# Loading v through a cast into SBUF per row tile, and the weights in ten pieces, in a top-k attention and MLP-mixer kernel

## The chip, the cores and the metric

The kernel runs on one core of a Trainium2 chip. The metric is device time in microseconds of one execution: 942.34 us is the median of three runs of the kernel before (939.85, 942.34 and 950.61). Profiles are of one execution each, on that core.

## What is computed

Eight batches of eight heads, 576 rows, 64 columns a head, in float32. Each row of scores keeps its 32 largest entries; the rest are masked out before the softmax. The attention output (576 x 512 per batch) goes through an MLP mixer.

```python
scores = scale * np.matmul(q, k.transpose(0, 1, 3, 2))
kth = np.partition(scores, -top_k, axis=-1)[..., -top_k:-top_k + 1]
scores = np.where(scores >= kth, scores, -1000000000.0)
attn = np.exp(scores - np.max(scores, axis=-1, keepdims=True))
attn = attn / (np.sum(attn, axis=-1, keepdims=True) + 1e-09)
x = np.matmul(attn, v)          # (8, 8, 576, 64), then (8, 576, 512)
h = np.maximum(x.transpose(0, 2, 1) @ w_tok1, 0.0) @ w_tok2
u = x + h.transpose(0, 2, 1)
out = u + np.maximum(u @ w_ch1, 0.0) @ w_ch2
```

## The kernel before

**Units and tiles.** The work is cut into 32 units; a unit is one pair of heads of one batch, four units make a batch. The 576 rows are four full row tiles of 128 and one of 64; with two heads a unit has nine score tiles of 128 x 576 (the two short ones share a tile). They are worked on in two groups, g=0 with four tiles and g=1 with five.

**One unit.** q and k are loaded in float32 on SP's DMA queue (`load_one`, L280; the first unit's k on ScalarE's), transposed on TensorE (`qk_tr`, L308), copied by ScalarE (`qk_ev`). Score products follow (`s1_mm`, `s0_mm` L360 to L372, `st_mm`), ScalarE copies them to SS (L375 and others). VectorE then selects the 32nd largest of each row. It splits the 576 columns into maxima and minima of halves (`upper`, L406, then `split4`, L430 to L440), takes the top eight again and again (`top_round`, MAX8 at L451 and MATCH_REPLACE8 at L456), and ends with `low_round` (L470). Beside it GpSimd rebuilds the smaller half from integer bits in two steps (`both_bits` L413, `lower_bits` L421), which `low_round` needs. GpSimd also does the small `neg_max` (L496), `raise_kth` (L522, tile kbig), `keep_ends` (L478, L479), and `sink` (L536), which masks four of the nine tiles in place.

**From scores to O.** The masked tiles have to be transposed before the product with v. Four of a unit's tiles (0, 1, 4, 5) are "turned": ScalarE makes a steep mask (`steep`, L528), GpSimd subtracts it, ScalarE takes the exponential into a buffer pb (L510), and a DMA transpose on SP's queue turns it (`turn`, L541). The other five are transposed by TensorE products with an identity (L558 and L561) and copied out by ScalarE (L581 to L614). Then `o_mm` (L620 to L632) makes O = P v for each head; v has a column of ones, so O's last column is the softmax denominator. VectorE takes its reciprocal (`o_den`, L638), and ScalarE or VectorE scales O into Xb (L648, L657). O has one bank, so the second head's product waits for the first head's scaling.

**The mixer.** After each unit the token mixing follows for its 128 channels (`h1_mm` L668, `ut_mm` L689). After each batch come the hidden products (`h2_mm` L723, `h2t_mm` L739, against wc1b) and the output products (`out_mm` L764, against wc2b), evacuated by ScalarE (L730, L745, L772) and stored by SP (L778). They are spread among the units of the next batch. The last batch has its own version (L1109 on).

**v and the weights.** For each batch one DMA on GpSimd's queue casts v from DRAM to a bf16 copy v16 in DRAM (`vconv`, L302); for each unit three DMAs on SP bring the pair's part of it into one of three buffers vb. The weights are cast into SBUF by GpSimd DMAs (`plan_weights`, L792): w1 and w2 together, wc1 in two halves of 768 KB, wc2 in two halves of 768 KB, each tied to the end of GpSimd's bit steps of an early half-unit (L911 to L914).

**What sets the order.** Each engine works through its instructions in program order. That order is made when the kernel is built: `Plan` (L36) simulates the engines with a fixed cost for each task (`dur`), waits (`deps`), buffers (`acq`, `rel`) and extra delays (`slack`); of the tasks that are ready on an engine it takes the one with the smallest `prio`, which is the unit's number times 100 plus an entry of `RANK` (L19). Entries ending in `_wait` are delays in tenths of a microsecond. `port` marks tasks that it keeps from running at once on VectorE and GpSimd. Where it finds TensorE idle it adds unread products into a free bank (`spare`, L265, 0.22 us planned for each 512 columns, L106 to L116):

```python
at, r, i = min(idle) if idle else (now, "", 0)
n = int((now - at) * SPARE / SPARE_US)
```

The times of the plan are not measured times; only the order of the instructions goes into the program.

## Time and profile before

| what | value |
| --- | --- |
| median of three runs | 942.34 us (939.85 to 950.61) |
| the profiled execution's own time | 944.13 us |
| its span, first to last instruction | 942.3 us |
| TensorE, VectorE, ScalarE, GpSimd busy | 861.9, 847.6, 846.3, 659.0 us |
| mean granted clock of TensorE | 0.973 |
| DMA queue of SP | 203,920 packets, 53.42 MB, 27.7% of 16 engines' span |
| DMA queue of GpSimd | 3,376 packets, 8.46 MB, 5.6% |

PE is TensorE, PEld its weight loads, DVE VectorE, ACT ScalarE, POOL GpSimd, SP SyncE; a q behind a name is that engine's instruction queue. `out<-in` names tiles written and read. In a timeline a row has the start, the length, the instruction and, in brackets, how long the engine stood idle before it and what ended that. In the chain of waits a row has the start, the share of the path in us, and what it was spent on. In a table by stretches each engine has its busy time and, in parentheses, the instructions that touch the stretch; then come the granted clock, the share of the DMA engines and GB/s. A group's row has count, busy time and mean (or shortest, median and longest) duration in ns.

### The profile page before, as it was taken

The numbers are of one execution on the slowest core, as the hardware profiler recorded it, in microseconds if no ns is written. First come the engines' busy times: TensorE is split into PE (matmuls) and PEld (weight loads), VectorE is DVE, ScalarE is ACT, GpSimd is POOL, SyncE is SP. The second block draws the span as 40 slices with busy tenths as digits, with TensorE's granted clock in tenths as the row PEclk, the third lists the DMA queues.
The fourth block names the chain that finished last, engine by engine and source line by source line (L and its number), as shares of the span: only waits on it lengthen the run. The fifth ranks groups of instructions, "written<-read, shape, count | busy, mean of one in ns | idle before, by whom it ended". The sixth has DMA issues, their size and how long they took to land.

```text
span 942.3 us, 22686 instructions
## 1 busy us (share of the span) xinstructions
PE 861.9 (91%) x7559; PEld 486.3 (52%) x7660; DVE 847.6 (90%) x3767; ACT 846.3 (90%) x1873; POOL 659.0 (70%) x542
## 2 busy tenths in 40 slices
PE   8979999899998999899998999899998999989896
PEld 6657555445553555455554455545554555545452
DVE  3987999899997999979997999979998899999852
ACT  3786899899998999899998999989998999999772
POOL 1984767788686778858677777867678577785800
PEclk9998999999998999899998999989998999999999
DMA  3494823334332232413324233412325232121101
GB/s 76 80 126 96 114 42 80 66 71 95 66 65 42 66 82 64 86 36 79 85 53 73 65 83 78 77 30 65 98 60 75 50 75 63 42 33 43 55 15 54
DMA packets 208621, 63.70 MB, mean 68 GB/s; under 512 B 200752, under 2 KB 203120, under 8 KB 208240
## 3 DMA queue, kind: packets, MB, share of 16 engines
q1 hardware_dynamic: 203920, 53.42, 27.7%
q0 software_dynamic: 3376, 8.46, 5.6%
q8 instruction: 62, 1.02, 0.4%
q14 instruction: 63, 0.52, 0.2%
q10 hardware_dynamic: 1200, 0.30, 0.2%
HBM read 40.50 MB, written 14.16 MB: 58 GB/s over the span
## 4 chain that ended last, share of the span: by engine, by line
ACT 41%; PE 23%; DVE 19%; POOL 11%; issue 3%; DMA 2%; ACTq 0%; DVEq 0%; SPq 0%
ACT U L528 6%; ACT SS L375 5%; ACT E L510 5%; DVE A L451 5%; PE s L365 5%; POOL kbig L522 4%; ACT pb L510 4%; ACT U L552 4%; DVE hx L456 4%; ACT pt L581 3%; ACT H2T L730 3%; ACT xb L648 3%; PE mps L764 3%; PE mps L723 3%; DVE A L470 3%
## 5 line engine op out<-in xcount | busy, mean ns | idle before, releaser
L413 POOL TENSOR_TENSOR lo<-SS 128x1152 int32<-128x1152 int32 x64 | 169.0, 2641 | 150.5 <-DVE A L451 132.2
L451 DVE MAX8 A<-hx 128x8 f32<-128x72 f32 (+2 forms) x1152 | 269.6, 292 | 0.0
L456 DVE MATCH_REPLACE8 hx<-A,hx 128x72 f32<-128x72 f32 (+1 forms) x864 | 199.0, 240 | 0.0
L365 PE MATMUL s<-qkT 64*128 64x512 f32 x512 | 171.0, 668 | 4.0 <-ACT SS L355 2.1
L421 POOL TENSOR_TENSOR lo<-lo,hi 128x1152 int32<-128x1152 int32 x64 | 169.2, 2643 | 0.0
L536 POOL TENSOR_TENSOR SS<-SS,U 128x576 f32<-128x576 f32 x126 | 159.1, 1287 | 0.0
L522 POOL TENSOR_SCALAR kbig<-A 128x4 f32<-128x4 f32 (+1 forms) x63 | 101.8, 1616 | 81.3 <-DVE A L470 68.2
L375 ACT COPY SS<-s 128x512 f32<-128x512 f32 x256 | 144.3, 627 | 15.3 <-PE s L365 15.3
L561 PE MATMUL tp<-identN,U 128*128 128x128 bf16 (+1 forms) x810 | 115.9, 220 | 16.1 <-ACT U L552 14.0
L510 ACT ACTIVATE E<-SS,nmax 128x576 bf16<-128x576 f32 x162 | 127.3, 825 | 0.2 <-POOL nmax L496 0.2
L552 ACT ACTIVATE U<-SS,A 128x576 bf16<-128x576 f32 x157 | 126.3, 838 | 0.0
L558 PE MATMUL tp<-identB,E 128*128 128x128 bf16 (+1 forms) x810 | 121.9, 222 | 4.5 <-ACT pt L585 2.0
L558 PEld LDWEIGHTS <-E 128*128 128x128 bf16 (+1 forms) x810 | 78.3, 100 | 77.3 <-issue 67.9
L470 DVE MAX8 A<-lo 128x8 f32<-128x296 f32 x288 | 116.9, 451 | 0.2
L528 ACT ACTIVATE U<-SS,kbig 128x576 bf16<-128x576 f32 x126 | 93.2, 810 | 23.0 <-POOL kbig L522 23.0
L406 DVE TENSOR_TENSOR hi<-SS 128x1152 f32<-128x1152 f32 x64 | 98.1, 1533 | 16.8 <-ACT SS L375 15.0
L723 PE MATMUL mps<-UT,wc1b 128*128 128x512 bf16 x323 | 90.4, 411 | 19.1 <-ACT H2T L745 15.7
L764 PE MATMUL mps<-wc2b,H2T 128*128 128x512 bf16 (+1 forms) x406 | 102.7, 380 | 4.1 <-issue 4.0
L510 ACT ACTIVATE pb<-SS,nmax 128x576 bf16<-128x576 f32 x126 | 102.9, 828 | 0.0
L561 PEld LDWEIGHTS <-U 128*128 128x128 bf16 (+1 forms) x810 | 80.0, 100 | 35.4 <-ACT U L552 26.4
L365 PEld LDWEIGHTS s<-qkT 64*128 64x128 f32 x512 | 54.2, 192 | 53.4 <-issue 31.7
L269 PEld LDWEIGHTS <-identB 128*128 128x128 bf16 x862 | 60.7, 102 | 38.2 <-issue 12.7
(121 smaller groups left out, 1577.5 us busy)
## 6 DMA issues: line engine op xcount, KB each, us to landing
qL<-in_q_dram SPq DMA_DIRECT2D x64, 128.0 KB, 2.6
kL<-in_k_dram SPq DMA_DIRECT2D x62, 128.0 KB, 2.7
out_dram<-ob SPq DMA_DIRECT2D x28, 256.0 KB, 2.3
v<-in_v_dram POOLq DMA_DIRECT2D x8, 576.0 KB, 7.5
vb<-v SPq DMA_DIRECT2D x64, 64.0 KB, 2.3
pt<-pb SPq DMA_TRANSPOSE x126, 2.4
wc1b<-in_moe_w_ch_dram POOLq DMA_DIRECT2D x2, 768.0 KB, 10.6
wc2b<-in_moe_w_ch_dram POOLq DMA_DIRECT2D x2, 768.0 KB, 8.5
```

The costliest lines, as they stand in the source:

```text
L365: nc.tensor.matmul(out=x[:, :], lhsT=T[rows[hh], 0, t * P : (t + 1) * P], rhs=T[rows[hh], 1, 0:W], start=True, stop=True,)
L375: nc.scalar.copy(out=st["SS", t // 2][:, 2 * (t % 2) + hh, 0:W], in_=st["s0", t][hh][:, :])
L413: nc.gpsimd.tensor_tensor(out=x[:, 0:4, 0:HALF].bitcast(i32), in0=SS[:, 0:4, 0:HALF].bitcast(i32), in1=SS[:, 0:4, HALF:S].bitcast(i32), op ...
L421: nc.gpsimd.tensor_tensor(out=x, in0=x, in1=st["hi"][:, 0:4, :].bitcast(i32), op=ALU.subtract)
L451: nc.vector.max(A[:, i, at], hx[:, i, 0:w])
L456: nc.vector.match_replace(hx[:, i, 0:w], A[:, i, TOP[r] : TOP[r] + 8], hx[:, i, 0:w], NEG)
L510: nc.scalar.activation(out=x, in_=srow(st, i), func=AF.Exp, bias=st["nmax", g][:, a : a + 1], scale=scale,)
L528: nc.scalar.activation(out=U[:, :], in_=srow(st, i), func=AF.Relu, bias=st["kbig", g][:, a : a + 1], scale=-STEEP,)
L536: nc.gpsimd.tensor_tensor(out=x, in0=x, in1=st["U", i][:, :], op=ALU.subtract)
L552: nc.scalar.activation(out=U[:, :], in_=srow(st, i), func=AF.Relu, bias=kcol(st, i), scale=-1.0)
L558: nc.tensor.matmul(out=out, lhsT=st["E", i][:, cols], rhs=identB[:, :], start=True, stop=False)
L561: nc.tensor.matmul(out=out, lhsT=st["U", i][:, cols], rhs=identN[:, :], start=False, stop=True)
```

## The change

- v is cast on its way from DRAM straight into SBUF, a row tile for all eight heads at a time (`v_piece`), by five DMAs per batch on GpSimd's queue. The copy in DRAM and the loads on SP go. There are two buffers vb, each for a batch.
- The weights come in ten pieces instead of five: w1 (two DMAs), w2, wc1 in four quarters, wc2 in four quarters, 384 KB each.
- All these DMAs are tied to the end of `upper`, the first step of a half-unit's selection: up to three v pieces of batch 0 and w1 in unit 0, one weight piece per half from unit 1 to unit 5's first half, and one v piece per half in the two units ahead of a batch and its first half.
- They have `port=False`, so the plan lets them run beside VectorE.
- The hidden products wait for wc1's pieces alone, the output products for wc2's.
- `LEAD` (4.6) replaces 0 as the time from which a bank counts as free at the start of the plan.
- Four buffers pb instead of five, one output buffer ob instead of two.
- Every entry of `RANK` that the plan uses has a new value but `o_wait`; `v_wait` is no longer used.

The fallback for rows with ties (behind the flag at the end) loads v with q's and k's buffers and copies it; it runs only if the flag is set. The diff, cut:

```diff
 RANK = {
-    "o_wait": 14, "t_wait": 0, "q_wait": 78, "v_wait": 112, "pre_mm": -2463, "pre_ev": -2226, "rest_mm": -3389, "begin": 9355,
...
-    "pt_tr0": -3127, "pt_tr1": -4980, "pt_ev0": 863, "pt_ev1": 4668, "o_mm0": -122, "o_mm1": 366, "o_ev0": -9780, "o_ev1": 4185,
+    "o_wait": 14, "t_wait": 1, "q_wait": 0, "v_wait": 112, "pre_mm": 820, "pre_ev": -3505, "rest_mm": -5033, "begin": 8436,
...
 }
 SPARE_US = 0.22
+LEAD = 4.6
...
-    def add(self, eng, dur, prio, fn, deps=(), acq=(), rel=(), slack=0.0, port=False):
+    def add(self, eng, dur, prio, fn, deps=(), acq=(), rel=(), slack=0.0, port=None):
         t = Task()
         t.eng, t.dur, t.prio, t.fn, t.acq, t.rel, t.slack = eng, dur, prio, fn, acq, rel, slack
         t.succ, t.nd, t.ready, t.seq = [], 0, 0.0, len(self.tasks)
-        t.port = port or eng == "POOL"
+        t.port = (eng == "POOL") if port is None else port
...
-        freed = {r: [0.0] * n for r, n in self.bufs.items()}
+        freed = {r: [LEAD] * n for r, n in self.bufs.items()}
...
-    outp = pool("outp", 2)
+    outp = pool("outp", 1)
     psum = pool("psum", 1, space=PS)
-    v16 = pool("dram", 1, space=bass.MemoryType.DRAM).tile([B, H, S, D], bf16, name="v16", tag="v16")
...
-    NVB = 3
+    NVB = 2
     vbufs = [
-        const.tile([P, NS, 2, D1], bf16, name=f"vb{i}", tag=f"vb{i}") for i in range(NVB)
+        const.tile([P, NS, H, D1], bf16, name=f"vb{i}", tag=f"vb{i}") for i in range(NVB)
...
-    NP = 5
+    NP = 4
...
     def load_one(st, name, src, b, p, queue=None):
         queue = queue or nc.sync
-        if name == "v":
-            src = v16
-            st["vb"] = take("vb", vbufs)
-            t = st["vb"][:, :, :, 0:D]
-        else:
-            t = ldp.tile([P, NS, 2, D], f32, name=name + "L", tag=name + "L")
+        t = ldp.tile([P, NS, 2, D], f32, name=name + "L", tag=name + "L")
...
-    def vconv(b):
+    def v_piece(mst, b, t):
+        if t == 0:
+            mst["vb"] = take("vb", vbufs)
+        m = csz(t)
         nc.gpsimd.dma_start(
-            out=v16[b, :, :, :].rearrange("h s d -> (h s) d"),
-            in_=v[b, :, :, :].rearrange("h s d -> (h s) d"),
-        )
+            out=mst["vb"][0:m, t, :, 0:D],
+            in_=v[b, :, t * P : t * P + m, :].rearrange("h p c -> p h c"),
+        )
...
-    def o_mm(st, hh, wide=False):
+    def o_mm(st, mst, p, hh, wide=False):
...
-                    rhs=st["vb"][:, j, hh, :],
+                    rhs=mst["vb"][:, j, 2 * p + hh, :],
...
-            E=5, U=8, P=NP, A=3, nmax=3, kbig=3, PT=2, Xb=2, H1T=2, UT=2, H2T=1, ob=2, den=4,
+            E=5, U=8, P=NP, A=3, nmax=3, kbig=3, PT=2, Xb=2, H1T=2, UT=2, H2T=1, ob=1, den=4,
...
-    def plan_weights():
-        tasks = {}
-
-        def piece(names, moves, prio):
-            def ld():
-                for src, dst in moves:
-                    m, r = divmod(src.shape[0], P)
-                    nc.gpsimd.dma_start(
-                        out=dst[:, 0:m, :], in_=src[0 : m * P, :].rearrange("(t p) c -> p t c", p=P)
-                    )
-                    if r:
-                        nc.gpsimd.dma_start(out=dst[0:r, m, :], in_=src[m * P :, :])
-
-            a = add("POOL", 1.2 * len(moves), prio, ld)
-            held.append(a)
-            x = add("DQ", 0.0, 0, lambda: None, deps=[a], slack=10.0)
-            for n in names:
-                tasks[n] = x
-
-        piece(["w1", "w2"], [(moe_w_tok1, w1b), (moe_w_tok2, w2b)], 30)
-        hc = NC // 2
-        for i in range(2):
-            piece(
-                [("c1", i)],
-                [(moe_w_ch1[i * hc * P : (i + 1) * hc * P, :], wc1b[:, i * hc : (i + 1) * hc, :])],
-                210 + i,
-            )
-        hf = NF // 2
-        for i in range(2):
-            piece(
-                [("c2", i)],
-                [(moe_w_ch2[i * hf * P : (i + 1) * hf * P, :], wc2b[:, i * hf : (i + 1) * hf, :])],
-                220 + i,
-            )
-        return tasks
-
-    conv = {}
-    held = []
-    wt = plan_weights()
+    slots = {}
+    wt = {}
+
+    def piece(u, g, name, fn, n=1):
+        slots.setdefault((u, g), []).append((name, fn, n))
+
+    def weight(src, dst):
+        m, r = divmod(src.shape[0], P)
+        nc.gpsimd.dma_start(out=dst[:, 0:m, :], in_=src[0 : m * P, :].rearrange("(t p) c -> p t c", p=P))
+        if r:
+            nc.gpsimd.dma_start(out=dst[0:r, m, :], in_=src[m * P :, :])
+
+    NQ = 4
+    c1, c2 = [("c1", i) for i in range(NQ)], [("c2", i) for i in range(NQ)]
+    piece(0, 1, "w1", lambda: weight(moe_w_tok1, w1b), 2)
+    piece(1, 0, "w2", lambda: weight(moe_w_tok2, w2b))
+    for i, at in enumerate(((1, 1), (2, 0), (2, 1), (3, 0))):
+        x, y = i * NC // NQ, (i + 1) * NC // NQ
+        piece(*at, c1[i], lambda x=x, y=y: weight(moe_w_ch1[x * P : y * P, :], wc1b[:, x:y, :]))
+    for i, at in enumerate(((3, 1), (4, 0), (4, 1), (5, 0))):
+        x, y = i * NF // NQ, (i + 1) * NF // NQ
+        piece(*at, c2[i], lambda x=x, y=y: weight(moe_w_ch2[x * P : y * P, :], wc2b[:, x:y, :]))
+    for b in range(B):
+        for t in range(NS):
+            at = (0, t // 3) if b == 0 else (NPAIR * b - 2 + t // 2, t % 2)
+            piece(*at, ("v", b, t), lambda b=b, t=t: v_piece(msts[b], b, t))
+    issue = {}
+    for at in sorted(slots):
+        for name, fn, n in slots[at]:
+            acq = [("vb", name[1])] if name[0] == "v" and name[2] == 0 else []
+            y = add("POOL", 0.65 * n, 100 * at[0] - 1200, fn, deps=[wt.get("first")], acq=acq, port=False)
+            wt["first"] = y
+            issue.setdefault(at, []).append(y)
+            wt[name] = add("DQ", 0.0, 0, lambda: None, deps=[y], slack=8.0)
...
-        if p == 0:
-            conv[b] = add("POOL", 1.0, U - 350 if b else 40, lambda: vconv(b), deps=[conv.get(b - 1), lobs.get((u - NPAIR + 1, 0))])
-            if b == 0:
-                held.insert(0, conv[b])
-            conv[b, "in"] = add("DQ", 0.0, 0, lambda: None, deps=[conv[b]], slack=10.0)
-        for name, src in (("q", q), ("k", k), ("v", v)):
+        for name, src in (("q", q), ("k", k)):
             aside = u == 0 and name == "k"
             ld[name] = add("ACT" if aside else "SP", 1.75, U + RANK["load"],
                            lambda name=name, src=src, aside=aside: load_one(st, name, src, b, p, nc.scalar if aside else None),
-                           deps=[conv[b, "in"]] if name == "v" else [],
-                           acq=[("vb" if name == "v" else "ld" + name, u)])
-        vc = add("DQ", 0.0, 0, lambda: None, deps=[ld["v"]], slack=4.5 if u < 4 else 0.1 * RANK["v_wait"])
+                           acq=[("ld" + name, u)])
...
             x = add("DVE", 0.305 * n + 0.035, U + 5 * g, lambda g=g: upper(st, g), deps=evs + [chain.get("bits")], port=True)
+            for y in issue.get((u, g), []):
+                pl.after(y, x)
             x = add("DVE", (2.13, 2.87)[g], U + 5 * g, lambda g=g: split4(st, g), deps=[x, chain.get("low")], port=True)
             lob = add("POOL", 2.6, U - 1000, lambda g=g: both_bits(st, g), deps=[x])
             lob = add("POOL", 2.6, U - 1000, lambda g=g: lower_bits(st, g), deps=[lob])
             nms[g] = chain["bits"] = lobs[u, g] = lob
-            if u < 3:
-                for t in held[:1]:
-                    pl.after(t, lob)
-                    held.remove(t)
             chain["first"] = smm[-1:] if u < 3 else []
...
-            om = add("PE", 1.01, V + RANK["o_mm" + str(hh)], lambda hh=hh: o_mm(st, hh, last),
-                     deps=[vc, None if last else oe] + tails + [PTd[i] for i in range(NTILE) if i == 2 * NT or i % 2 == hh],
-                     acq=[O], rel=[("PT", u), ("vb", u)] if hh else [])
+            om = add("PE", 1.01, V + RANK["o_mm" + str(hh)], lambda hh=hh: o_mm(st, mst, p, hh, last),
+                     deps=[wt["v", b, t] for t in range(NS)] + [None if last else oe] + tails + [PTd[i] for i in range(NTILE) if i == 2 * NT or i % 2 == hh],
+                     acq=[O], rel=([("PT", u)] if hh else []) + ([("vb", b)] if hh and p == NPAIR - 1 else []))
...
-        wl = [wt[n, i] for n in ("c1", "c2") for i in range(2)]
+        wl = [wt[n] for n in c1]
...
-                        deps=hs + oms[-1:], acq=[] if part else [("mps", b, "o", sc)],
+                        deps=hs + oms[-1:] + [wt[n] for n in c2], acq=[] if part else [("mps", b, "o", sc)],
...
-                        deps=mst["ute"] + wl, acq=[("mps", b, "h2", fc)])
+                        deps=mst["ute"] + [mst["pres"][fc]], acq=[("mps", b, "h2", fc)])
```

23 lines of the change are left out of this document (16 added, 7 removed), and 7 rows, old and new, of the table RANK.

## The prediction

> **What bounds the kernel now.** I read the page's head first, then the busy time by stretches, what sat idle on VectorE, the chain of waits, and only then the rows of the operations that the edit touches.
>
> ```profile
> span 942.3 us, 22686 instructions
> PE 861.9 (91%) x7559; PEld 486.3 (52%) x7660; DVE 847.6 (90%) x3767; ACT 846.3 (90%) x1873; POOL 659.0 (70%) x542
> ```
>
> Three engines are about 90% busy, so shares do not say which one rules. The next view gives busy time in four stretches, each from the start of one unit's selection to the next unit's (a unit is one pair of heads).
>
> ```profile
> core 0: us, PE busy (x) PEld busy (x) DVE busy (x) ACT busy (x) POOL busy (x), PEclk, DMA share, GB/s
> 18.80:44.20 25.40, 23.27 (x229) 14.70 (x228) 25.36 (x115) 18.18 (x37) 20.01 (x13) 1.00 0.31 60
> 44.20:79.80 35.60, 28.83 (x363) 22.93 (x361) 25.92 (x117) 23.33 (x48) 23.78 (x23) 0.90 0.93 129
> 298.40:324.00 25.60, 24.79 (x177) 12.76 (x178) 25.57 (x117) 25.60 (x59) 20.04 (x16) 1.00 0.30 63
> 376.00:407.60 31.60, 27.09 (x250) 14.52 (x251) 26.02 (x119) 26.92 (x60) 22.54 (x17) 0.89 0.36 66
> ```
>
> VectorE does 25.4 to 26.0 us of work in every unit, and a good unit lasts no longer than that: 25.57 busy of 25.60. So VectorE's selection is the floor, and time is lost only where VectorE stands still: 9.7 us in unit 1 (35.60 less 25.92) and 5.6 us in unit 13 (31.60 less 26.02). What it stood still for:
>
> ```profile
>   PE O L626: 49.6, 16
> ```
>
> ```profile
> 73.02 0.20 DVE L638 RECIPROCAL rden<-O 128x5 f32<-128x5 f32 x1 [6.99 <-PE O L626]
> ...
> 79.69 0.20 DVE L638 RECIPROCAL rden<-O 128x5 f32<-128x5 f32 x1 [2.65 <-PE O L626]
> ```
>
> ```profile
> 405.57 0.20 DVE L638 RECIPROCAL rden<-O 128x5 f32<-128x5 f32 x1 [5.51 <-PE O L626]
> ```
>
> All of it is one instruction: the reciprocal of the softmax denominator stands in VectorE's in-order queue and waits for the attention-times-v product O, 49.6 us in 16 waits. 9.64 us of these (6.99 + 2.65) fall in unit 1; 5.51 is the wait of unit 13. The chain of waits says why, and what happens before the first selection.
>
> ```profile
> 3.83 8.16 PE O L269 x108
> ...
> 57.58 14.21 DMA pt<-pb
> ```
>
> ```profile
> 387.60 0.53 POOL v L303
> ...
> 388.20 4.24 POOL kbig L522
> ```
>
> At first TensorE runs 108 unread products (8.16 us) and the real work stands behind them. In unit 1 the chain passes through a DMA transpose that takes 14.21 us to land. In unit 13 it passes through the small multiply kbig on GpSimd, 4.24 us long, and then through TensorE and ScalarE to O, which is ready some 13 us after kbig's end (at 405.57, by the row above).
>
> **The change part by part.**
>
> *Fewer unread products at first.* The planner pads an idle TensorE from the time a bank is taken to be free; that becomes 4.6 instead of 0. Before, 108 products are int(7.45 x 0.8 / 0.22) = 27 groups of four; 7.45 is its own 1.75 + 1.2 + 4.5 for q's load. With 4.6 it is int(2.85 x 0.8 / 0.22) = 10 groups, 40 products. Are they hiding a load? And how long are 40?
>
> ```profile
> kL<-in_k_dram ACTq DMA_DIRECT2D x1, 32.0 KB, 4.0
> ```
>
> ```profile
> 1.89 0.70 ACTq L297 DMA_DIRECT2D kL<-in_k_dram  x1
> ```
>
> ```profile
> 4.00:5.00 1.00, 1.00 (x12) 1.00 (x11) 1.00 1.36 205
> 4.00:7.00 3.00, 3.00 (x31) 3.00 (x30) 1.00 1.17 188
> 9.00:10.00 1.00, 1.00 (x22) 1.00 (x20) 1.00 0.00 0
> 9.00:11.00 2.00, 2.00 (x40) 2.00 (x38) 1.00 0.03 8
> ```
>
> The last piece of k is there at 1.89 + 4.0 = 5.9 us, so after that the products hide nothing. The last fence counts them: 19 more in 2 us early (105 ns each), 18 more in 1 us later (56 ns each). Solving 8.16 us for a mix gives some 40 slow ones, so 40 products last about 4.2 us, to 8.0. Gain 3.9 us, all of it ahead of the first selection, on the chain. What could spoil it: the real work up to the first selection (18.80 less 11.99, 6.8 us, about half of it TensorE's) would fall partly into the slow spacing, at the ratio 105 to 56 at most some 3 us. I take 3.9, since 40 products just cover the slow stretch; range 1 to 3.9. The profile's granted clock shows 1.00 in both stretches, yet the products' own spacing halves. [...]
>
> *Weights in smaller pieces at other times, v by row tile.* Eight DRAM-to-DRAM casts of v, 96 loads of the cast copy (three per unit, on SP) and four large weight loads go. Forty casts straight into SBUF and eleven weight DMAs come, all in GpSimd's queue, each placed behind the first step of a half-unit's selection. Their cost at issue:
>
> ```profile
> L799 POOL DMA_DIRECT2D wc1b<-in_moe_w_ch_dram x2: 765/791/817, 58.0 to 68.2; - x2
> L799 POOL DMA_DIRECT2D wc2b<-in_moe_w_ch_dram x2: 909/916/922, 93.1 to 103.9; - x2
> L799 POOL DMA_DIRECT2D w1b<-in_moe_w_tok_dram x1: 871/871/871, 42.6 to 42.6; - x1
> ```
>
> ```profile
> 93.22 0.92 DVE L434 TENSOR_TENSOR lo<-hi 128x720 f32<-128x720 f32 x1
> ```
>
> These move 256, 768 and 512 separate rows (128 partitions by 2, 6 and 4). A v piece moves 128 x 8 = 1024 rows: estimate 0.97 us, the line through 0.79 and 0.92 carried on; bounds 0.6 (as small as the old v cast) and 1.3. Forty are 39 us of GpSimd time, against eight old ones; GpSimd has 283 us idle, and the place is a good one:
>
> ```profile
> L413 POOL TENSOR_TENSOR lo<-SS 128x1152 int32<-128x1152 int32 x64 | 169.0, 2641 | 150.5 <-DVE A L451 132.2
> ```
>
> It stands idle 150.5 / 64 = 2.35 us ahead of each of its first bit step L413, just where the pieces go. One piece hides there: cost 0. In the first unit there are three in one half (2.9 us) and w1's two with two v pieces in the other (about 3.3 us): 0.6 and 0.9 us too much. How much spare time GpSimd's result has is seen in the same unit, on GpSimd and on VectorE:
>
> ```profile
> 25.33 2.63 POOL L421 TENSOR_TENSOR lo<-lo,hi 128x1152 int32<-128x1152 int32 x1
> ```
>
> ```profile
> 28.48 0.45 DVE L470 MAX8 A<-lo 128x8 f32<-128x296 f32 x1
> ```
>
> It ends at 27.96 and is read at 28.48: 0.5 us to spare in a first half; a second half has a fifth tile on VectorE and so more. I put 0.7 us on VectorE, range 0 to 1.5.
>
> Does VectorE's two-input work hold such an issue up, as it holds kbig? The first wc2b issue, at 93.1, ran beside the L434 above, the second at 103.9 did not, and they took 909 and 922 ns: no. [...]
>
> *What the pieces collide with.* The 14.21 us transpose was issued at 57.58 and one 768 KB piece at 58.0, the next at 68.2. The usual and the disturbed landing of a transpose:
>
> ```profile
> DMA to landing us min/median/max: 2.4/2.4/14.2
> ```
>
> ```profile
> DMA to landing us min/median/max: 2.8/5.0/7.2
> ```
>
> The first is over all 126; the second is of the two in the stretch from 496 to 504 us, just behind a 576 KB v cast. The new pieces are 256 to 384 KB, nearest to the second row: I take 7.2. With 3.9 us from the start, the transposes of unit 0 go out at about 53.7 or earlier (the weight issues ahead of that kbig go too) and land by 60.9; O follows 1.1 us later, at 62.0. VectorE would ask at 73.02 - 6.99 - 3.9 = 62.1. So both waits of unit 1 go: gain 9.6 us (0 if a new piece holds the transpose as long as the old one did). What is late next is nothing that the rows show within a few microseconds: ScalarE and TensorE stood idle in the same stall (23.33 of 35.60 busy). In later batches five v pieces per batch may meet transposes, where one cast did; the cast at 387.60 had a pair right behind it as well, and O was due only at 405.57 - 5.51 = 400.1, 12 us after. Cost 0, bound 2 us.
>
> *Weights later, and waited for apart.* The hidden products now wait for c1 alone, the output products for c2.
>
> ```profile
> L739 PEld LDWEIGHTS <-wc1b x384: 95/98/98, 166.2 to 916.5; 128*128 128x128 bf16 x192
> ```
>
> ```profile
> L764 PE MATMUL mps<-wc2b,H2T x406: 377/379/403, 198.8 to 890.9; 128*128 128x512 bf16 x108, 128*64 128x512 bf16 x28
> ```
>
> Unit 2 began at 79.8, will begin some 12 us earlier, and a unit lasts about 26 us: the last of c1 goes out in unit 3 (about 95 us), the last of c2 in unit 5 (about 150); even with 14.2 us, the worst landing above, they are there some 45 and 20 us ahead of the first use (166.2 and 198.8, less the 12). Cost 0.
>
> *Fewer buffers.* Four transposing buffers instead of five, one output buffer instead of two.
>
> ```profile
> L541 SPq DMA_TRANSPOSE pt<-pb x126: 1199/1224/5134, 43.0 to 895.9; - x126
> ```
>
> ```profile
> out_dram<-ob SPq DMA_DIRECT2D x28, 256.0 KB, 2.3
> ```
>
> ```profile
> L772 ACT COPY ob<-mps x5: 603/642/691, 318.7 to 362.9; 128x512 f32<-128x512 f32 x4, 64x512 f32<-64x512 f32 x1
> ```
>
> 126 transposes in 853 us are one per 6.8 us, so a buffer of four comes round after 27 us and has landed in 2.4. Output copies come 11 us apart and their store lands 2.3 us after its issue. Both cost 0. SP loses 96 issues; no engine waited for v's loads, so that gives 0 too. The first wait that a v piece has on GpSimd is for its buffer, last read by O two batches earlier: long done.
>
> *The order.* Every rank of the table changes, and three of the planner's artificial delays. No row prices this. Upward: three of four units are already at VectorE's floor, and only the late O of one unit per batch can go, at most 49.6 - 9.6 = 40 us. Downward: each further late O like unit 13's costs 5.5 us a batch, 38 over seven. I take 0, by the nearest row, the good unit (25.57 of 25.60), which has nothing to gain.
>
> **Sum** against the profiled execution, which took 944.1 (span 942.3): 944.1 - 3.9 - 9.6 + 0.7 = 931.3. It is 1.8 above the median of the three runs, 942.3; against the median 929.5, say 930.
>
> **Rivals.**
>
> *The late O of each batch shrinks as well.* The v cast at 387.60 leaves the queue ahead of kbig, and the order is new. For: kbig's 4.24 us are mostly a wait behind VectorE's two-input steps, and the shortest of its 63 takes 0.23:
>
> ```profile
> L522 POOL TENSOR_SCALAR kbig<-A x63: 227/1337/4449, 30.2 to 879.7; 128x4 f32<-128x4 f32 x32, 128x5 f32<-128x5 f32 x31
> ```
>
> Against: the cast is 0.53 us, and kbig can not start before VectorE's own last step anyway. Half of the 5.5 us in six batches is 16 us, all 33: 914 to 897.
>
> *The transpose stall stays.* A 384 KB piece of c1 goes out within 2 us of unit 0's last transposes. If it holds them the full 14.2 us, only the 3.9 us are won, and small new waits eat some of it: 939.
>
> *Slower: a second late O in each batch.* The new order puts O behind the hidden-layer products in another unit, VectorE stands 5.5 us once more per batch: 930 + 6 x 5.5 = 963. Above 2 us per batch the start's gain is gone; above 3.6 us it is slower by more than 1%. For: O stands behind some 13 us of other work in unit 13, and every rank moves. Against: three of four units show no such wait now.
>
> **How the numbers follow.** 1% is about what a measurement of this kernel can tell. Sum as above: 0.40 (925 to 937). Late O shrinks: 0.22. Stall stays or as much is lost elsewhere: 0.18 (933 to 952). Second late O: 0.20. Faster than 932.9: 0.22 and most of the first, 0.36, so 0.58. Within 1%: 0.04 + 0.18 = 0.22. Slower: 0.20. The range from 904 to 955 leaves out the full removal of the late O (0.05) and most of the slower case (0.14). The likeliest case's own range is 925 to 937.
>
> **What would show it.** Forty products and the first VectorE step L406 at about 15 us instead of 18.81; unit 1 in some 26 us, no wait of the reciprocal above 2 us before 80 us; no transpose landing later than 8 us; wc1b landing before its first use with no wait; L413 with a piece ahead of it and its idle time smaller, with L470 not waiting for GpSimd. I am wrong if the reciprocal's waits add up to more than 40 us, if L470 waits for GpSimd, or if ScalarE waits for ob or pb.

## The result, and the profile after

| | before | after |
| --- | --- | --- |
| median, with one more run of before beside the kernel after | 945.05 us (939.85 to 950.61, 4 runs) | 913.73 us (912.24 to 915.79, 4 runs) |
| profiled execution: its time, span | 944.1, 942.3 us | 915.8, 914.0 us |
| first selection begins | 18.81 us | 16.15 us |
| mean granted clock of TensorE | 0.973 | 0.987 |

The ratio after to before is 0.967 (95% interval 0.960 to 0.974): 31 us won, where 12.3 were forecast (942.3 less 930). The direction was right and 913.73 lies in the range of 904 to 955, but more than half of the gain has another source than the sum named.

The head of the page of the kernel after, to be held against the two lines that the prediction begins with:

```profile
span 914.0 us, 22276 instructions
PE 834.9 (91%) x7408; PEld 474.4 (52%) x7510; DVE 848.8 (93%) x3766; ACT 842.4 (92%) x1873; POOL 690.3 (76%) x576
```

VectorE does the same work in both (847.6 and 848.8 us). TensorE is busy 27 us less, in part because 150 unread products are gone (862 weight loads of them before, 712 after), 68 of them at the start, for the rest because its products run faster (mean granted clock 0.973 and 0.987): shares of busy time hide that. Busy time by stretches, after: unit 0, unit 1, unit 3, a good unit (unit 10) and unit 13.

```profile
core 0: us, PE busy (x) PEld busy (x) DVE busy (x) ACT busy (x) POOL busy (x), PEclk, DMA share, GB/s
16.15:42.51 26.36, 24.22 (x213) 14.34 (x212) 25.40 (x114) 17.62 (x36) 20.33 (x13) 0.94 0.31 42
42.51:68.74 26.23, 25.83 (x337) 19.95 (x335) 26.20 (x117) 23.45 (x51) 22.84 (x21) 1.00 0.51 82
94.78:125.89 31.11, 26.25 (x197) 13.71 (x197) 26.23 (x120) 22.80 (x48) 25.87 (x22) 0.89 0.42 52
287.97:313.57 25.60, 24.00 (x177) 12.75 (x179) 25.48 (x116) 25.60 (x61) 19.66 (x16) 1.00 0.44 63
366.17:392.90 26.73, 23.68 (x242) 14.35 (x244) 26.02 (x118) 25.59 (x58) 22.60 (x18) 1.00 0.23 48
```

Unit 1 has gone from 35.60 to 26.23 us, as forecast. Unit 13 has gone from 31.60 to 26.73, with the same VectorE work (26.02): that was not forecast. Unit 3 is new: 31.11, with the granted clock at 0.89. What VectorE waited for at the reciprocal, after (49.6 us before):

```profile
  PE O L633: 24.6, 18
```

The starts of the units (the first step of each selection on VectorE, taken from the timelines of both) show where the 28.3 us between the two spans went:

| stretch | before | after | change |
| --- | --- | --- | --- |
| up to the first selection | 18.81 | 16.15 | -2.7 |
| unit 0 | 25.34 | 26.36 | +1.0 |
| unit 1 | 35.65 | 26.23 | -9.4 |
| units 2 to 5 | 107.5 | 112.3 | +4.8 |
| units 6 to 27 | 600.1 | 579.6 | -20.5 |
| the rest | 154.9 | 153.4 | -1.5 |

The first three rows are the sum of the prediction, forecast as -3.9, +0.7 and -9.6. What its order term, taken as 0, has to answer for is rows four and five, 15.7 us net. The rows come from one profiled execution of each kernel.

### What makes O late in each batch

The timeline of the kernel before, all engines, around unit 13 (the first selection step L406 of its second half began at 387.81):

```profile
388.20 4.23 POOL L522 TENSOR_SCALAR kbig<-A 128x4 f32<-128x4 f32 x1
392.46 1.44 ACT L528 ACTIVATE U<-SS,kbig 128x576 bf16<-128x576 f32 x2 [1.82 <-POOL kbig L522]
393.81 0.85 ACT L745 ACTIVATE H2T<-mps 128x512 bf16<-128x512 f32 x2
394.44 1.86 PE L723 MATMUL mps<-UT,wc1b 128*128 128x512 bf16 x4 [2.83 <-ACT H2T L745]
396.24 2.08 PE L365 MATMUL s<-qkT 64*128 64x512 f32 x4
398.60 1.89 PE L723 MATMUL mps<-UT,wc1b 128*128 128x512 bf16 x4
400.42 1.16 PE L365 MATMUL s<-qkT 64*128 64x512 f32 x4
...
404.48 1.05 PE L626 MATMUL O<-vb,pt 128*128 128x65 bf16 x25
```

kbig, a multiply of 512 numbers, is held on GpSimd until VectorE's two-input steps are done (the last of them ends at 392.34, kbig at 392.43). ScalarE's queue has the steep step (L528, which needs kbig) at its head, so ScalarE stands for 1.82 us. The H2T eviction (L745) stands behind it, and TensorE's hidden products need the bank that it frees: TensorE stands for 2.83 us. Then come four hidden products in 1.86 us, and four score passes in 2.08, where the same work takes about half further down (1.16 at 400.42). So O starts at 404.48. The slow stretch stands in the granted clock too, if the window is cut to it (columns as above):

```profile
394.40:400.40 6.00, 5.96 (x14) 1.52 (x13) 5.66 (x34) 4.09 (x9) 6.00 (x5) 0.50 0.19 35
```

The 0.89 of the whole unit is this stretch averaged over 31.60 us: 0.11 x 31.60 x 2 is some 7 us at half the clock. The same stretch of the kernel after (that selection step, now L413, began at 377.97):

```profile
378.14 4.44 POOL L529 TENSOR_SCALAR kbig<-A 128x4 f32<-128x4 f32 x1
379.96 0.89 ACT L752 ACTIVATE H2T<-mps 128x512 bf16<-128x512 f32 x2
380.63 1.89 PE L730 MATMUL mps<-UT,wc1b 128*128 128x512 bf16 x7 [1.67 <-ACT H2T L752]
382.62 0.78 ACT L535 ACTIVATE U<-SS,kbig 128x576 bf16<-128x576 f32 x1 [1.10 <-POOL kbig L529]
...
388.12 1.04 PE L730 MATMUL mps<-UT,wc1b 128*128 128x512 bf16 x4
...
391.71 1.04 PE L633 MATMUL O<-vb,pt 128*128 128x65 bf16 x25
...
392.79 0.20 DVE L645 RECIPROCAL rden<-O 128x5 f32<-128x5 f32 x1 [0.64 <-PE O L633]
```

```profile
380.60:390.00 9.40, 8.79 (x50) 4.06 (x51) 9.40 (x55) 8.30 (x18) 9.32 (x6) 1.00 0.31 66
```

kbig is held just as long. But the new order has H2T ahead of the steep step, TensorE stands for 1.67 us only, the granted clock stays at 1.00, and seven products take 1.89 us where four took 1.86. O comes 13.7 us behind the selection step rather than 16.7, and the reciprocal waits 0.64 us rather than 5.51.

### The profile page after: what moved, and what is told of

Its sections match the earlier page's. It is cut to its first block, busy times and chain, and to the rows that moved or that the text cites. A ratio compares the mean times of both kernels' runs of the same rounds, so it can differ in the third digit from the quotient of the medians.

```text
span 914.0 us, 22276 instructions
## 1 busy us (share of the span) xinstructions
PE 834.9 (91%) x7408; PEld 474.4 (52%) x7510; DVE 848.8 (93%) x3766; ACT 842.4 (92%) x1873; POOL 690.3 (76%) x576
## 3 DMA queue, kind: packets, MB, share of 16 engines
q1 hardware_dynamic: 165520, 48.69, 26.5%
## 4 chain that ended last, share of the span: by engine, by line
ACT 41%; DVE 34%; PE 13%; POOL 7%; issue 4%; DMA 0%; SPq 0%; ACTq 0%; DVEq 0%; POOLq 0%
DVE A L458 9%; DVE hx L463 8%; ACT SS L382 7%; ACT U L535 5%; ACT U L559 5%; ACT E L517 5%; DVE A L477 5%; POOL kbig L529 4%; DVE hi L413 4%; ACT pb L517 4%; ACT H2T L737 3%; ACT pt L588 2%; DVE lo L441 2%; DVE hx L441 2%; ACT xb L655 2%
## 5 line engine op out<-in xcount | busy, mean ns | idle before, releaser
L372 PE MATMUL s<-qkT 64*128 64x512 f32 x512 | 164.4, 655 | 6.8 <-ACT SS L362 4.9
L382 ACT COPY SS<-s 128x512 f32<-128x512 f32 x256 | 148.9, 670 | 7.5 <-PE s L372 7.3
L529 POOL TENSOR_SCALAR kbig<-A 128x4 f32<-128x4 f32 (+1 forms) x63 | 96.2, 1527 | 51.4 <-DVE A L477 37.4
L517 ACT ACTIVATE E<-SS,nmax 128x576 bf16<-128x576 f32 x162 | 134.1, 879 | 0.2 <-POOL nmax L503 0.2
L559 ACT ACTIVATE U<-SS,A 128x576 bf16<-128x576 f32 x157 | 130.4, 879 | 0.0
L535 ACT ACTIVATE U<-SS,kbig 128x576 bf16<-128x576 f32 x126 | 101.2, 854 | 19.8 <-POOL kbig L529 19.8
L413 DVE TENSOR_TENSOR hi<-SS 128x1152 f32<-128x1152 f32 x64 | 99.0, 1548 | 11.7 <-ACT SS L382 11.7
L517 ACT ACTIVATE pb<-SS,nmax 128x576 bf16<-128x576 f32 x126 | 106.7, 883 | 2.5 <-POOL SS L543 2.5
L730 PE MATMUL mps<-UT,wc1b 128*128 128x512 bf16 x313 | 82.4, 383 | 15.2 <-ACT H2T L752 10.4
L588 ACT ACTIVATE pt<-tp 128x512 bf16<-128x512 f32 x130 | 81.6, 670 | 0.0
L269 PEld LDWEIGHTS <-identB 128*128 128x128 bf16 x712 | 49.5, 100 | 50.1 <-issue 26.8
```

The source lines that it names most:

```text
L372: nc.tensor.matmul(out=x[:, :], lhsT=T[rows[hh], 0, t * P : (t + 1) * P], rhs=T[rows[hh], 1, 0:W], start=True, stop=True,)
L382: nc.scalar.copy(out=st["SS", t // 2][:, 2 * (t % 2) + hh, 0:W], in_=st["s0", t][hh][:, :])
L517: nc.scalar.activation(out=x, in_=srow(st, i), func=AF.Exp, bias=st["nmax", g][:, a : a + 1], scale=scale,)
L559: nc.scalar.activation(out=U[:, :], in_=srow(st, i), func=AF.Relu, bias=kcol(st, i), scale=-1.0)
```

## The experiments

Theory A: the order is what won the time in the batches, and the new transfers of v do nothing there. Rivals: the transfers of v (the cast that left kbig's neighbourhood), or the place of the reciprocal in VectorE's own queue. Each ratio is to the kernel before, run on the same chip.

### The order and the transfers apart

*The kernel after with the old order table.*

```diff
-    "o_wait": 14, "t_wait": 1, "q_wait": 0, "v_wait": 112, "pre_mm": 820, "pre_ev": -3505, "rest_mm": -5033, "begin": 8436,
...
-    "h2_ev": 2782, "h2t_mm": -322, "h2t_ev": 1399, "pret_mm": -777, "pret_ev": -1881, "accum": 3779, "s_mm0": -1988, "s_mm1": -6875,
...
+    "o_wait": 14, "t_wait": 0, "q_wait": 78, "v_wait": 112, "pre_mm": -2463, "pre_ev": -2226, "rest_mm": -3389, "begin": 9355,
...
+    "h2_ev": 144, "h2t_mm": -2857, "h2t_ev": -1227, "pret_mm": -3806, "pret_ev": -2151, "accum": -358, "s_mm0": -3924, "s_mm1": -3851,
...
```

> The changed kernel with the old table of ranks: all new transfers, buffers and LEAD, but the order planned with the old ranks and waits. Theory A (the order won the batches: with the new ranks the reciprocal asks for O later and O comes earlier): the late O comes back, several us per batch, so 935 to 950 us, only the start's few us won. Theory B (the transfers won them: no v cast ahead of kbig, no v loads on SP): 912 to 920 us, as the changed kernel.

Measured: 955.5 us, ratio 1.012 (1.004 to 1.020): the new transfers in the old order are slower than the kernel before, more so than theory A gave. The row of the selection's first step, of this kernel:

```profile
L413 DVE TENSOR_TENSOR hi<-SS 128x1152 f32<-128x1152 f32 x64 | 98.4, 1538 | 33.7 <-ACT SS L382 22.3 <-ACT SS L402 11.4
```

VectorE stands 33.7 us ahead of it until ScalarE has copied scores, against 11.7 in the kernel after (all of them the start), and the reciprocal's waits are 38.6 us. By stretches, the first selection begins at 16.31 and unit 1 takes 26.90 us, so the gains of the start and of unit 1 do not need the new order table. Units 2 to 5 take 131.5 us (107.5 before, 112.3 after), units 6 to 27 take 594.1 (600.1 and 579.6), the rest 159.6. So of the 20.5 us won in units 6 to 27 the table carries 14.5; 6.0 come without it. And in units 2 to 5 the rest of the change needs it: without it 24.0 us are lost, with it 4.8.

*The kernel after with the old transfers of v*, in the new order and with the new weight pieces:

```diff
-        m = csz(t)
-        nc.gpsimd.dma_start(
-            out=mst["vb"][0:m, t, :, 0:D],
-            in_=v[b, :, t * P : t * P + m, :].rearrange("h p c -> p h c"),
-        )
+            nc.gpsimd.dma_start(
+                out=v16[b, :, :, :].rearrange("h s d -> (h s) d"),
+                in_=v[b, :, :, :].rearrange("h s d -> (h s) d"),
+            )
...
+    def v_pair(mst, b, p):
+        t = mst["vb"][:, :, 2 * p : 2 * p + 2, 0:D]
+        rws = v16[b, 2 * p : 2 * p + 2, :, :]
...
+            nc.sync.dma_start(
+                out=t[:, 0:NT, hh, :], in_=rws[hh, 0:W, :].rearrange("(t p) c -> p t c", p=P)
+            )
```

> The changed kernel's plan and order, but v takes the old way: one DRAM to DRAM cast per batch where its first piece stood, nothing in the place of the other four, and three loads per unit on SP behind the first step of the unit's second half. Theory A (order): 912 to 920 us. Theory B (transfers): most of the gain goes, 932 to 942 us.

Measured: 911.95 us, ratio 0.965 (0.957 to 0.973). The new transfers of v, after which the change is named, won nothing in the new order: without them the kernel is as fast. The fourth corner, the new table in the kernel before as it stands, was not run.

*The v cast of the kernel before moved away from kbig*, half a unit later:

```diff
-            conv[b] = add("POOL", 1.0, U - 350 if b else 40, lambda: vconv(b), deps=[conv.get(b - 1), lobs.get((u - NPAIR + 1, 0))])
+            conv[b] = add("POOL", 1.0, U - 350 if b else 40, lambda: vconv(b) if b == 0 else None, deps=[conv.get(b - 1), lobs.get((u - NPAIR + 1, 0))])
...
-            lob = add("POOL", 2.6, U - 1000, lambda g=g: lower_bits(st, g), deps=[lob])
+            lob = add("POOL", 2.6, U - 1000, lambda g=g: (lower_bits(st, g), vconv(b + 1) if g and p == 1 and b < B - 1 else None), deps=[lob])
```

> The kernel before, same plan; the v cast of batches 1 to 7 stands on GpSimd half a unit later, behind the bit steps, so not ahead of kbig. If the cast ahead of kbig makes kbig late (theory B, part): kbig in unit 13 falls from 4.2 to 1.5 us or less, O comes 2 to 3 us earlier, 925 to 932 us. If kbig is held by VectorE's two-input steps anyway: kbig still about 4.4 us and the time within 2 us of before.

Measured: 938.3 us, ratio 0.993 (0.990 to 0.996). In unit 13 kbig still takes 4.45 us with no cast ahead of it, and the reciprocal waits 5.29. So a gain was measured where within 2 us of before was expected for this case; it is in unit 1, 27.9 us long instead of 35.6, while unit 3 is 3.3 us longer. In unit 1 of the kernel before a cast (issued at 57.42, landed 8.5 us later), a transpose (57.58, 14.2 us) and a weight piece (58.03, 13.6 us) are under way at once; here the cast goes out half a unit later. The transposes' landing in this kernel, from 57 to 72 us (in the kernel before 11.7 to 14.2):

```profile
DMA to landing us min/median/max: 5.9/8.0/8.4
```

### What the late O consists of

*The kernel before with the reciprocal of the first head placed later in VectorE's queue*, behind the last selection step, for the O of each batch's first unit (unit 12's O is the one that unit 13 waits for):

```diff
-            r = add("DVE", 0.08, U - 500, lambda hh=hh: o_den(st, hh), deps=[om], acq=[("den", u, hh)],
+            r = add("DVE", 0.08, U - 500, lambda hh=hh: pend.append((st, hh)) if hh == 0 and p == 0 else o_den(st, hh), deps=[om], acq=[("den", u, hh)],
```

> The kernel before, same plan and order on TensorE, GpSimd and SP; only the reciprocal for the first head of a batch's first unit stands on VectorE behind the low round (some 2 us of VectorE work) instead of ahead of it, or as far back as its reader allows. If VectorE's place for the reciprocal makes the loss: the 5.5 us waits fall to about 3.5 and each batch is 2 us shorter, 930 to 933 us in all. If TensorE and ScalarE bound that unit whatever VectorE does: the wait moves and the time stays within 2 us.

Measured: 943.7 us, ratio 0.999 (0.995 to 1.002). The wait of unit 13 falls from 5.51 to 3.51 us, and two units later new waits of 1.5 and 0.4 us give the 2 us back. VectorE's place is not the cause.

*The kernel before with two steps of ScalarE's queue exchanged*: in the second unit of batches 2 and later the steep steps stand behind H2T (`flush`, put at the end of `h2t_ev`, issues those that `pend` holds back).

```diff
-        )
+        ); flush() if fcs[0] else None
...
-                    m = add("ACT", 0.67, V + RANK["steep" + str(g)] + i, lambda i=i: steep(st, i), deps=[kb, chain.get("steep")], acq=[("U", u, i)])
+                    m = add("ACT", 0.67, V + RANK["steep" + str(g)] + i, lambda i=i: pend.append((st, i)) if p == 1 and i < 4 and 1 < b else steep(st, i), deps=[kb, chain.get("steep")], acq=[("U", u, i)])
```

> The kernel before, with one thing of ScalarE's order alone changed: in the second unit of batches 2 and later, the two steep steps (which need kbig) stand behind the two H2T evictions instead of ahead of them. TensorE's, VectorE's and SP's order stay. Theory C (what makes the late O of each batch is that kbig's hold by VectorE reaches TensorE by way of ScalarE's queue, steep first and H2T behind it): kbig is still held for about 4.4 us in unit 13, but TensorE's idle 2.8 us at 394 shrinks below 1.7, its products there take about 1.0 us for four rather than 1.86, the reciprocal's wait in that unit falls from 5.5 to 0 to 1.5, and the batch from 109.2 to about 105: some 4 us in each of five batches, 918 to 925. Rival (steep's own followers, sink and the exponential, carry the hold to the same O): the wait in unit 13 stays at 4 us or more, 938 to 944.

Measured: 927.2 us, ratio 0.986 (0.981 to 0.992). Its timeline around unit 13:

```profile
383.36 4.24 POOL L522 TENSOR_SCALAR kbig<-A 128x4 f32<-128x4 f32 x1
385.62 0.89 ACT L745 ACTIVATE H2T<-mps 128x512 bf16<-128x512 f32 x2
386.89 1.03 PE L723 MATMUL mps<-UT,wc1b 128*128 128x512 bf16 x4
387.63 1.44 ACT L528 ACTIVATE U<-SS,kbig 128x576 bf16<-128x576 f32 x2 [1.12 <-POOL kbig L522]
...
396.94 0.20 DVE L638 RECIPROCAL rden<-O 128x5 f32<-128x5 f32 x1 [1.70 <-PE O L626]
```

kbig is held as before, TensorE's wait of 2.83 us is gone, four products take 1.03 us, and the reciprocal waits 1.70 us. Unit 13 is 27.8 us instead of 31.6. Two steps in each of five units carry 3.8 of the 4.9 us that the kernel after wins in that unit. Wait and time fell a little less than expected. The run does not separate the shorter wait from the pace that follows it; the next one does.

*The kernel before with the idle time filled*: twelve unread products ahead of each batch's first hidden products, and no other change.

```diff
-        ps = bank("mps")
+        ps = bank("mps"); [spare("O", 0, 1, 100.0) for _ in range(12 if fc == 0 else 0)]
```

> The kernel before, with twelve unread 512-wide products (about 2.6 us at 0.215 each) put ahead of each batch's first hidden product, where TensorE stood idle for 2.8 us; nothing else changes, and the work is still held up as before. Theory K (of the late O, the slow clock that follows the idle time is the larger part): the four hidden products there take about 1.0 us rather than 1.86, O in unit 13 comes 2 to 3 us earlier, the wait of 5.5 falls to about 3, and the batch loses 1 to 2 us: 930 to 937. Rival (ScalarE's late start is all of it, and the products after it wait for ScalarE at either clock): wait still 5 us or more, 942 to 948.

Measured: 929.45 us, ratio 0.986 (0.981 to 0.992). Its timeline:

```profile
391.41 2.98 PE L269 MATMUL O<-w1b,identB 128*128 128x512 bf16 x13
392.33 1.44 ACT L528 ACTIVATE U<-SS,kbig 128x576 bf16<-128x576 f32 x2 [1.82 <-POOL kbig L522]
393.68 0.85 ACT L745 ACTIVATE H2T<-mps 128x512 bf16<-128x512 f32 x2
394.30 1.02 PE L723 MATMUL mps<-UT,wc1b 128*128 128x512 bf16 x4
...
402.63 0.20 DVE L638 RECIPROCAL rden<-O 128x5 f32<-128x5 f32 x1 [2.70 <-PE O L626]
```

```profile
394.30:400.40 6.10, 6.10 (x35) 2.25 (x35) 5.63 (x34) 6.08 (x15) 6.10 (x5) 1.00 0.19 35
```

ScalarE waits as long as before (1.82), and the hidden products start no earlier (6.6 us behind the selection step in both, which here began at 387.68). Yet they take 1.02 us rather than 1.86, at a granted clock of 1.00 rather than 0.50, and the reciprocal waits 2.70 rather than 5.51. So 2.8 us, half of the reciprocal's wait, was TensorE's slower pace after the idle time, and no wait that a chain of releasers could show.

### The start

*The kernel after with the old rule for the unread products* (`LEAD = 0.0`), and *the kernel before with the new one* (4.6 in the list of times at which banks are free).

> The changed kernel with LEAD at 0: 108 unread products at the start again, all else the same instructions in the same order. If the 68 products stand on the path: 68 x 56 ns = 3.8 us less what the first transposes win by a faster clock (0.4), so first selection 3.4 us later and 917 us. If something else holds the start (loads): no change, 914 us.

> The kernel before with 40 unread products at the start and nothing else changed. If the start shifts everything: first selection at 15.4 to 15.6 us instead of 18.81 and the time 3.3 us lower. If the stall of unit 1 (a transpose that lands late) takes it up again: the same time within 1 us, unit 1 longer by 3 us.

Measured: 917.4 us, ratio 0.972 (0.965 to 0.980), with the first selection at 19.14; and 938.8 us, ratio 0.996 (0.993 to 0.999), with the first selection at 14.47. The edit is worth 3.0 us of the start in the kernel after and 4.3 in the kernel before, a microsecond more than expected there. The start of the kernel after:

```profile
0.92 1.04 DVE L235 MEMSET vb<- 64x520 bf16 x2 [0.92 <-PEq L1303]
...
3.96 0.48 DVE L259 MEMSET O<- 128x512 f32 x1
4.50 4.42 PE L269 MATMUL O<-identB 128*128 128x128 bf16 x40 [4.50 <-DVE O L259]
...
8.72 1.06 PE L319 MATMUL tp<-identF,qL 128*128 128x128 f32 x4
...
16.15 1.36 DVE L413 TENSOR_TENSOR hi<-SS 128x1152 f32<-128x1152 f32 x1 [11.70 <-ACT SS L382]
```

The two buffers for a whole batch are larger, their clears take 1.04 us of VectorE, and the clear of O's bank, which the products wait for, ends at 4.44 us; the products began at 3.83 before. The 40 products take 4.42 us, and the first transposes 1.06 against 0.61 where the products went on to 12 us: in this execution they end before TensorE is at full pace. In the kernel before with 40 products they take 3.83 us from 3.83 on, and the first transposes 0.61: there TensorE was at full pace by then.

*The kernel after with O's bank cleared first on VectorE*:

```diff
+    bankO = psum.tile([P, 512], f32, name="O0", tag="O0")
+    nc.vector.memset(bankO[:, :], 1.0)
...
-    nc.vector.memset(banks["O"][0][:, :], 1.0)
```

> The changed kernel with the clear of O's bank as VectorE's first instruction, so that the 40 unread products begin some 2.5 us earlier. If the products hold the start and q and k are there: first selection at 13.4 to 14 us instead of 16.15 and 911 us. If the loads or the clock hold it: first selection no more than 1 us earlier, 913 us.

Measured: 910.8 us, ratio 0.964 (0.960 to 0.970), first selection at 13.39. The products begin at 1.72, and the first selection 2.8 us earlier. The time is 2.9 us below that of the kernel after, but on another chip, and the intervals of the two ratios overlap.

### The size of the weight pieces, and a faster version

*The kernel after with wc1 and wc2 in pieces of 768 KB*, every second issue left out and the one before it doubled:

```diff
-        piece(*at, c1[i], lambda x=x, y=y: weight(moe_w_ch1[x * P : y * P, :], wc1b[:, x:y, :]))
+        y += y - x
+        piece(*at, c1[i], (lambda: None) if i % 2 else (lambda x=x, y=y: weight(moe_w_ch1[x * P : y * P, :], wc1b[:, x:y, :])))
```

> The changed kernel's plan, but wc1 and wc2 come in two pieces of 768 KB each, at the first and third of their four places. If the size of the piece made the transpose of 14 us (the prediction's step): transposes of unit 0, issued beside the first piece, land 10 us or later again, VectorE waits for O in unit 1 or 2, and the time is 3 to 8 us higher, 917 to 922. If the new order leaves O enough room: no wait above 1 us in units 1 and 2 and 912 to 916 us.

Measured: 912.3 us, ratio 0.966 (0.961 to 0.971). A transpose now lands up to 10.3 us after its issue, and units 1 and 2 do not stall for it (26.2 and 26.5 us). What the new plan does for unit 1 is not to make the pieces small. Unit 3 is 26.1 us long here, without the new wait; the last part of this section comes back to that.

*Both of the last two edits*:

> The kernel after, with the two edits that each gained: O's bank is cleared first on VectorE (first selection about 13.4 us instead of 16.2) and wc1 and wc2 come in pieces of 768 KB rather than 384. If the gains add, 908 to 910; if the stall of unit 3 or unit 5 comes back at other places, 911 to 914.

Measured: 911.3 us, ratio 0.967 (0.961 to 0.974). The gains do not add; the new waits of units 3 and 5 stay (30.6 and 29.3 us). *The same with 15 unread products at one place in unit 3*, between the two halves of a score product:

```diff
         for hh in range(2):
+            if t == 2 and hh == 1:
+                seen.append(t)
+                spare("O", 0, 15 if len(seen) == 5 else 0, 100.0)
             x = bank("s0")
```

> The run before this one (the kernel after with O's bank cleared first and larger pieces of wc1 and wc2), and beside it fifteen unread 512-wide products (15 x 0.215 = 3.2 us) at one place alone: in unit 3, between the two score products where TensorE stood idle for 3.25 us while kbig was held for 4.45 us. If the new wait of unit 3 is the same thing as the late O of each batch before, in smaller, the score products behind the place go at about 1.1 us for four rather than 2.08, the reciprocal's wait of 3.8 us there falls to 1 to 2, unit 3 is 28 to 29 us rather than 30.6, and the whole is about 2 us shorter: 907 to 910. Rival (ScalarE's late start alone makes that wait): unit 3 stays at 30 us or more, 910 to 913.

Measured: 905.8 us, ratio 0.961 (0.957 to 0.965), the lowest here; the interval overlaps with that of the run before it (0.961 to 0.974), which had another chip, so this gain is not clear of noise. Unit 3 without the 15 products, and then with them:

```profile
103.55 4.45 POOL L530 TENSOR_SCALAR kbig<-A 128x4 f32<-128x4 f32 x1
...
109.01 2.07 PE L373 MATMUL s<-qkT 64*128 64x512 f32 x2 [3.24 <-ACT SS L363]
...
112.83 2.01 PE L373 MATMUL s<-qkT 64*128 64x512 f32 x4
...
116.45 1.05 PE L634 MATMUL O<-vb,pt 128*128 128x65 bf16 x25
```

```profile
104.21 1.55 POOL L535 TENSOR_SCALAR kbig<-A 128x4 f32<-128x4 f32 x1
...
106.37 3.41 PE L270 MATMUL O<-w1b,identB 128*128 128x512 bf16 x14
109.71 1.12 PE L378 MATMUL s<-qkT 64*128 64x512 f32 x2
...
114.48 1.05 PE L639 MATMUL O<-vb,pt 128*128 128x65 bf16 x25
```

The first profile is the late O of the kernel before in another place: kbig, ScalarE, idle TensorE, slow products. From the first products shown on, TensorE is busy without a break in both, and O follows 7.44 us later without the fill and 4.77 with it. The pace alone gives those 2.7 us. But that the fill made the pace is not shown: in the second profile kbig happened to be held for 1.55 us only, so the idle time to be filled was not there. In the run with pieces of 768 KB kbig was short as well, with no fill (the selection step L413 of this half began there at 107.01, L419 here at 104.03):

```profile
107.18 1.55 POOL L529 TENSOR_SCALAR kbig<-A 128x4 f32<-128x4 f32 x1
...
109.75 1.12 PE L372 MATMUL s<-qkT 64*128 64x512 f32 x2 [0.34 <-ACT SS L362]
```

The same products start 2.7 us behind the selection step there and 5.7 with the fill, which stood in their way; unit 3 took 26.1 us there, 28.0 with the fill and 30.6 with the long kbig. So, as far as these three profiles show, unit 3 was shorter for the short hold of kbig, not for the fill. What makes the hold short in some of them stays open.

## Why the prediction was right in part and wrong in size

- **The start** (3.9, range 1 to 3.9): 2.7. The products themselves were sized rightly for the kernel before, where the edit alone gave 4.3. Two things took from it: the larger buffers' clears were not counted, 0.67 us ahead of the first product, and TensorE came to its full pace later than in that run (40 products in 4.42 us and not 3.83, the first transposes in 1.06 and not 0.61). The slow transposes stood in the prediction as the range's lower end.
- **Unit 1** (9.6): 9.4, and by the step named. No transpose lands later than 6.1 us there, 6.8 anywhere, and the reciprocal does not wait. The reason was half right: the stall does go when the transposes no longer meet both a weight piece and a v cast, but the pieces' size does not matter (768 KB pieces do as well), and either half of the meeting can go: with the cast moved alone unit 1 was 27.9 us, with the cast kept and the pieces at their new places 26.6. "What is late next is nothing that the rows show" was wrong: unit 3 stands 4.32 us and unit 5 3.3, and units 2 to 5 give back 4.8 us.
- **GpSimd's issues** (0.97 us each, 0.7 us on VectorE): right. Rows of the kernel after, first a v piece, then the idle time ahead of the first bit step, then VectorE's one wait for GpSimd:

```profile
L301 POOL DMA_DIRECT2D vb<-in_v_dram x40: 717/964/1122, 3.3 to 760.3; - x40
```

```profile
L420 POOL TENSOR_TENSOR lo<-SS 128x1152 int32<-128x1152 int32 x64 | 168.6, 2634 | 117.0 <-DVE A L458 101.6
```

```profile
40.56 0.47 DVE L477 MAX8 A<-lo 128x8 f32<-128x296 f32 x1 [0.92 <-POOL lo L428]
```

- **Buffers, and weights later** (0): right; nothing waited for ob, pb, wc1b or wc2b.
- **The order** ("I take 0, by the nearest row, the good unit (25.57 of 25.60), which has nothing to gain"): this is the step that failed. The good unit is the wrong row. The term belonged to the bad unit of each batch, 31.6 us, which is now 26.7; units 6 to 27 won 20.5 us, 14.5 of them by the table. In place of the row that has nothing to gain the runs showed a chain that an exchange of two ScalarE steps shortens: kbig's hold, ScalarE's queue, H2T, idle TensorE and then half the clock. The rival "the late O of each batch shrinks as well" (914 to 897, chance 0.22) is what happened. It named the right place and a size in its range; that 913.73 falls on its edge of 914 is in part luck, since 4.8 us were lost in units 2 to 5. And its first reason, the cast that leaves kbig's neighbourhood, is refuted: kbig's hold did not change, and moving the cast alone left the wait at 5.29 us.
- **The other rivals.** The transpose stall did not stay. A second late O came, but in units 3 and 5 once each, not in each batch: 4.8 us and not 33.
- **What the profile did show.** The rows at 392.46 to 398.60 above are in the trace of before: an engine's queue headed by a step that waits, the eviction behind it, a bank that TensorE needs, and products at half pace behind the idle time. The granted clock of 0.89 in unit 13 stood in the prediction's own table and was not asked about. By what filling the idle time won, that clock was worth 2.8 us in each of five batches.
- What stays open: why the old table with the new transfers is slower than with the old ones (955 against 942) is seen only as far as the 21.8 us that the selection waits for ScalarE's copies, in four waits of 3.7 to 7.6 us, all in units 2 to 5; which entry makes them was not tried. Which entries of the new table, beyond the two steps exchanged above, win the rest was not tried either.

## What to carry to other kernels

Before an order is priced at zero, follow the worst repeated wait back through every in-order queue: the cure may be two instructions exchanged on an engine that is not the bound. Where a stretch shows a granted clock under 1, compare the spacing of its products with the same products elsewhere; idle TensorE time of some 3 us ahead of a critical chain can be filled with unread products, and in the kernel before that alone won as much as the exchange (ratio 0.986 for each); where the idle time did not come, as in unit 3 of the last run, the fill delayed the work behind it. A late chain that goes away in one unit is to be looked for in the next ones.

## What the runs showed of the hardware

- **Pace after idle time.** Before, 2.83 us of idle TensorE were followed by products at half pace: 1.86 us for four against 1.02 to 1.04, at a granted clock of 0.50. (At the start of the kernel the clock reads 1.00 at either spacing, 105 and 56 ns, so there it does not show the pace.) After, 1.67 us of idle time at the same place of unit 13 were not. With 3.24 us, in unit 3 of the run with both edits, they were again (2.01 us for four score passes against 1.13 in the run with the 15 products). The length of one gap does not decide it: in the kernel after, 1.90 us that end at 33.3 us were followed by a granted clock of 0.50 from 33.9 to 37.2, and in its unit 9 the clock was 0.50 from 279.7 to 282.9, 6 us behind a gap of 1.67; that unit took 28.39 us, where units 13, 17, 21 and 25 took 26.7 to 26.8. What decides it, no run here shows.
- **kbig's hold.** The same multiply of 128 x 4 or 128 x 5 numbers takes 0.23 us at best, 1.34 in the median and 4.45 at most, in the kernels before and after alike. In the kernel before, 11 of its 63 executions last 4.19 to 4.45 us, and each of these ends 0.08 to 0.09 us behind the last of VectorE's six two-input steps (L406 to L438; 387.81 to 392.34 in unit 13, where kbig ends at 392.43). In 36 it lasts 1.27 to 1.55 us and ends 0.08 to 0.11 us behind the first of these steps (the two profiles above with 1.55 us are of this kind). The longest of the two-input steps of unit 13's second half took 1.64 us, so the hold of 4.23 us there went over several in a row.
